# Sliding-window attention with an MLP-Mixer on one core: more dummy products at the start, evictions that lean to ScalarE only later, and new orders of PE's work and of the loads

## The chip, the cores and the metric

The kernel runs on one core of one Trainium2 chip. The metric is the device time of one execution in microseconds (us). Engines are named as in the profile: PE (TensorE, matrix products), PEld (its weight loads), DVE (VectorE), ACT (ScalarE), POOL (GpSimd) and SP (SyncE, which here only issues transfers).

## The reference

Attention over a sliding window with sink keys, then one MLP-Mixer layer on the merged heads:

```python
scores = scale * np.matmul(q, k.transpose(0, 1, 3, 2))       # q, k, v: [4, 8, 768, 64], scale = 1/8
keep = is_sink | in_window                                   # keys 0 to 3, or 0 <= row - key < 128
scores = np.where(keep, scores, -1000000000.0)
a = np.exp(scores - np.max(scores, axis=-1, keepdims=True))
x = (a / np.sum(a)) @ v, heads merged                        # [4, 768, 512]
h = np.maximum(xt @ w_tok1, 0.0) @ w_tok2                    # xt = x transposed; w_tok1 [768, 256], w_tok2 [256, 768]
u = x + h.transpose(0, 2, 1)
out = u + np.maximum(u @ w_ch1, 0.0) @ w_ch2                 # w_ch1 [512, 1536], w_ch2 [1536, 512]
```

Inputs and outputs are FP32; the kernel computes its products in BF16 and adds in FP32.

## The kernel before

**Tiles and stages.** The 32 heads are worked off as 16 pairs of two heads; pairs 0 to 3 make batch 0, and so on. For one pair, q and k (128 partitions by 768) are turned, so that the head's 64 channels lie on partitions; scores of keys against the queries of their window are formed in three groups (each a tile of two PSUM banks), ACT takes the exponential of each group (L692), and the values product with v and a column of ones (`pv`, two halves of three tiles of queries) gives sums and outputs, which DVE normalizes into x_sb (reciprocal L778, product L781). The four sink keys of a pair have a product of their own (`score_sinks`, L746). When the four pairs of a batch are there, its tokens are mixed (`mix_h`, `mix_u`, with w_tok1 and w_tok2) to u, u is turned, and the channels are mixed (`mix_channels`), by a scheme of seven products for eight, whose sums of weights (L1484) DVE forms from w_ch. DVE evicts the output tiles (L1276), and SP and ACT store them (L1286).

**How q and k come in.** Pairs 0 to 3: SP loads them in FP32 (`load_raw`, L136, tiles q_f and k_f), and ACT, DVE or POOL casts them into q_bf and k_bf (`copy`, L195 on ACT, L197 on DVE and POOL). From pair 4 on POOL's own transfers cast on the way (`load_cast`, L168 and L173). Pairs 0 to 7 are turned on PE (L159 for batch 0, L163 for batch 1) and copied out of PSUM into qT and kT, by ACT or DVE, in two halves each; pairs 8 to 15 are turned by DMA transpositions that SP issues (L555). v of every pair comes by `load_v` (POOL, L181, six buffers v_aug in turn) and the weights by `load_w` (POOL, L206).

**Masks.** In the first pairs PE adds the mask to the scores (a product of mask_add and the identity, before the scores of the group); later DVE (L711) or POOL (L703) masks what ACT has written.

**What sets the order.** PE's order is written out in the table `ORDERED`, in words such as `s5`: a letter for a stream and a unit's number in it. t: turning q (even) and k (odd) of pairs 0 to 3; m: the mask products; s: the score groups of pairs 0 to 3 with the sink scores among them; o: the sink rows and `pv` halves of batch 0 (o1 and o2 are pair 0, o3 and o4 pair 1, o5 and o6 pair 2, o7 and o8 pair 3); g and h: token mixing of batch 0's two halves; a: score groups from pair 4 on (a12 is the first of pair 8); v: the `pv` halves of those; w: turning by PE from pair 4 on; k: token mixing from batch 1 on; n: sink scores of later pairs; c, x and y: the channel products. The table `LOADS` sets the order of POOL's loads: q, k and v with the pair, t with w_tok1 or w_tok2, c and d with a quarter of w_ch1 or w_ch2. All these loads go through one queue.

What ACT, DVE, POOL and SP do, and when, is decided as the program is built by a planner, class `Plan`: it keeps a time for each engine (`plan.free`), and for each pending operation a list of the engines that can do it, with a cost for each. `other` takes the operation that could begin first and gives it to the engine where its end, by these costs, is earliest; 400 ns (`BIAS`) are added against DVE, so that ACT is favoured. The order in which the planner takes operations is the order in which each engine has them in its queue. `commit_pe` and `choose` give each PE unit its PSUM banks, four single ones ("mx") and two double ones ("sc"); a unit of turning holds a bank until the copies that read it are done.

**The start.** The first instructions of DVE are memsets: the tile of the sink values (L219), the tile `ones` (L220), mask_add (L241). `ones` is the first 512 columns of a kT buffer and feeds seven dummy products of 128 by 512 (`keep_warm`), which begin before any data has arrived, and whose result nobody reads. POOL builds the identity and the masks (L243 to L255) and then issues the load of pair 0's v.

## Time and profile before

| | us |
|---|---|
| median of three runs | 191.21 (191.1 to 191.54) |
| the profiled execution | 191.41 |
| its span (first to last instruction) | 189.7 |
| mean granted clock of TensorE | 0.998 |
| PE busy | 181.5 |
| DVE, ACT, POOL busy | 160.8, 112.1, 78.5 |
| first dummy product, first transposition | 2.07, 5.17 |
| first exponential (ACT L692) | 8.45 |
| first product with v (o1) | 14.50 |
| last wait of PE over 0.2 before the end (for x_sb) | ends 28.45 |
| first scores of pair 8 (a12) | 63.59 |
| last product ends, about | 186.4 |

Busy shares say which engine has most to do, the windows where it has gaps, the waits what it waits for there, and the chain of work that ended last which of these waits counted. In the rows of the timeline the number in brackets is the idle time just before, and behind the arrow stands what ended it; "ps" is a bank of PSUM.

### The profile page before, as it was taken

Reading aid. Unit: us, or ns where it says so; the run is one execution under the profiler, and the core shown is the slowest. Engines: PE = TensorE matmul, PEld = TensorE weight load, DVE = VectorE, ACT = ScalarE, POOL = GpSimd, SP = SyncE. Lnnn points to the kernel's source line nnn. Section 1 sums busy time; section 2 is a strip of 40 time slices with the busy share of each in tenths; the row PEclk is TensorE's granted clock in tenths of the full one; section 3 lists DMA queues with packets and bytes.
Section 4 is the critical chain, followed back from the end, with each engine's and each line's share of the span. In section 5 each row is a group of like instructions: output and inputs, shape, how many; then the busy total and the mean of one; then the engine's idle time right before and its main releaser. Section 6 shows DMA issues by size and latency. Waiting matters only on the chain.

```text
span 189.7 us, 5560 instructions
## 1 busy us (share of the span) xinstructions
PE 181.5 (96%) x2269; PEld 131.7 (69%) x2269; DVE 160.8 (85%) x343; ACT 112.1 (59%) x210; POOL 78.5 (41%) x122
## 2 busy tenths in 40 slices
PE   5889989999999999999999999999999999999992
PEld 1335758766777888766666788865578887668882
DVE  4766969997699999988999998879998968799882
ACT  4698978999974653858875711488842203773000
POOL 5938566374807989472804970150240000000000
PEclk9999999999999999999999999999999999999999
DMA  5999999999999999999999995431100145200035
GB/s 186 288 276 185 188 193 199 200 197 178 175 141 119 168 117 158 135 149 170 292 119 147 166 117 117 180 146 28 28 5 0 28 86 221 111 0 3 0 138 194
DMA packets 82600, 26.31 MB, mean 139 GB/s; under 512 B 70032, under 2 KB 80272, under 8 KB 82576
## 3 DMA queue, kind: packets, MB, share of 16 engines
q0 software_dynamic: 56864, 11.80, 82.8%
q1 hardware_dynamic: 25088, 13.64, 33.0%
q10 hardware_dynamic: 624, 0.53, 0.8%
q8 instruction: 17, 0.28, 0.6%
q14 instruction: 7, 0.06, 0.2%
HBM read 26.75 MB, written 6.29 MB: 174 GB/s over the span
## 4 chain that ended last, share of the span: by engine, by line
PE 87%; DMA 5%; ACT 2%; DVE 1%; issue 1%; POOL 1%; POOLq 0%
PE ps L188 85%; DMA v_aug<-in_v_dram 5%; ACT pT L692 2%; PE ps L191 1%; PE ps L163 1%; DVE x_sb L781 1%; PE ps L597 1%; ACT kT L195 0%; POOL mask_add L247 0%; POOL mask_add L251 0%; DVE pT L711 0%; DVE o_sb L1276 0%; ACT u_sb L195 0%; DVE recip L778 0%; POOL ident L244 0%
## 5 line engine op out<-in xcount | busy, mean ns | idle before, releaser
L692 ACT ACTIVATE pT<-ps 128x1024 bf16<-128x1024 f32 (+1 forms) x48 | 44.9, 963 | 20.1 <-PE ps L188 19.8
L195 ACT ACTIVATE parts<-ps 128x384 f32<-128x384 f32 x54 | 24.6, 490 | 18.0 <-PE ps L188 16.5
L188 PE MATMUL ps<-uT,w_ch 128*128 128x384 bf16 x168 | 33.7, 326 | 0.0
L1164 DVE CUSTOM_DVE_ANT_0 v1T<-ps,parts 128x384 bf16<-128x384 f32 x54 | 28.1, 552 | 6.4 <-PE ps L188 6.0
L188 PEld LDWEIGHTS <-v1T 128*128 128x128 bf16 x288 | 27.6, 98 | 4.4 <-issue 0.2
L188 PEld LDWEIGHTS <-w_ch 128*128 128x128 bf16 x204 | 19.1, 98 | 10.7
L201 ACT ACTIVATE v1T<-ps 128x384 bf16<-128x384 f32 x41 | 19.8, 497 | 9.4 <-PE ps L188 8.8
L188 PE MATMUL ps<-uT_sums,k_f 128*128 128x384 bf16 x108 | 23.5, 326 | 0.0
L188 PEld LDWEIGHTS <-v_sums 128*128 128x128 bf16 x216 | 20.8, 98 | 3.4 <-issue 0.2
L703 POOL TENSOR_SCALAR_AFFINE_SELECT pT<-pT 128x256 bf16<-128x256 bf16 (+1 forms) x20 | 11.6, 612 | 24.4 <-issue 14.6
L188 PEld LDWEIGHTS <-w_tok 128*128 128x128 bf16 x192 | 18.1, 98 | 4.3 <-issue 1.3
L1276 DVE TENSOR_TENSOR o_sb<-ps,u_sb 128x512 f32<-128x512 f32 (+1 forms) x32 | 17.3, 551 | 3.2 <-PE ps L188 3.2
L188 PEld LDWEIGHTS <-k_f 128*128 128x128 bf16 x144 | 13.6, 98 | 8.3 <-issue 0.6
L188 PE MATMUL ps<-q_f,v1T 128*128 128x256 bf16 x144 | 19.0, 273 | 0.0
L188 PE MATMUL ps<-w_ch,v1T 128*128 128x256 bf16 x144 | 18.8, 273 | 0.0
L188 PE MATMUL ps<-q_f,v_sums 128*128 128x256 bf16 x144 | 18.7, 273 | 0.0
L188 PE MATMUL ps<-v_aug,pT 128*128 128x65 bf16 x352 | 17.7, 194 | 1.0 <-DMA v_aug<-in_v_dram 1.0
L188 PEld LDWEIGHTS <-pT 128*128 128x128 bf16 x352 | 16.2, 98 | 3.0 <-DMA v_aug<-in_v_dram 1.5
L181 POOL DMA_DIRECT2D v_aug<-in_v_dram x16 | 16.5, 1037 | 3.2 <-PE ps L188 1.5
L781 DVE TENSOR_TENSOR x_sb<-ps,recip 128x384 bf16<-128x384 f32 x32 | 17.2, 550 | 0.4
L188 PEld LDWEIGHTS <-kT 64*64 64x64 bf16 (+2 forms) x343 | 7.9, 104 | 13.0 <-issue 9.0
L188 PE MATMUL ps<-qT,kT 64*64 64x192 bf16 (+2 forms) x336 | 15.5, 249 | 0.3 <-ACT pT L692 0.3
(91 smaller groups left out, 301.4 us busy)
## 6 DMA issues: line engine op xcount, KB each, us to landing
v_aug<-in_v_dram POOLq DMA_DIRECT2D x16, 192.0 KB, 10.3
w_ch<-in_moe_w_ch_dram POOLq DMA_DIRECT2D x8, 384.0 KB, 10.9
out_dram<-o_sb SPq DMA_DIRECT2D x6, 512.0 KB, 2.9
out_dram<-o_sb SPq DMA_DIRECT2D x10, 256.0 KB, 2.2
q_f<-in_q_dram SPq DMA_DIRECT2D x4, 384.0 KB, 5.1
k_f<-in_k_dram SPq DMA_DIRECT2D x4, 384.0 KB, 5.8
k_bf<-in_k_dram POOLq DMA_DIRECT2D x16, 96.0 KB, 7.6
q_bf<-in_q_dram POOLq DMA_DIRECT2D x16, 96.0 KB, 10.5
```

Of the source, the lines that this page charges most:

```text
L163: issue(nc.tensor.transpose(outs[x][ds(D * h, D), j], t[rows, h, j], ident[rows, rows]))
L181: in_order(nc.gpsimd.dma_start(out=v_aug.rearrange("p i t d -> p (i t) d")[:, :, 0:D], in_=v[b].rearrange("h s d -> (h s) d")[2 * hp * S:2 ...
L188: issue(nc.tensor.matmul(*args, skip_group_check=True, **kwargs))
L191: issue(nc.tensor.transpose(out, in_, ident))
L195: in_order(nc.scalar.activation(out, in_, AF.Copy))
L201: in_order(nc.scalar.activation(out, in_, AF.Relu))
L597: issue(nc.tensor.transpose(outs[x][columns], rows_by_columns[rows, columns], ident[rows, rows]))
L692: in_order(nc.scalar.activation(part(tiles["pT", p][:, :, ds(2 * g, 2)]), of_keys(tiles["ps_s", p, g])[:, :, 0:width(g)], AF.Exp, scale=scale,
L703: in_order(nc.gpsimd.affine_select(out=pt, in_=pt, compare_op=ALU.is_ge, fill=0.0, base=-n, pattern=[[0, nk], [1 - 2 * n, P]], channel_mul ...
L781: in_order(nc.vector.tensor_tensor(out=x_sb[b][:, ts(half, QH), ts(hp, 2 * D)].rearrange("p t (i d) -> p t i d", i=2), in0=tiles["ps_o", p ...
L1164: in_order(nc.vector._custom_dve(TENSOR_ADD_SAT, out=v1_of(i, half), in0=ps, in1=kept[:, n], s0=HUGE, s1=0.0,))
L1276: in_order(nc.vector.tensor_tensor(out=sb(*out), in0=tiles["ps_out", b, t0, key[0]], in1=in1(), op=ALU.add,))
```

## The change

It has five parts.

1. The tile `ones` is filled first of all, in two memsets (128 columns, then 384), ahead of the tile of the sink values. The dummy products are eight of 128 columns and then seven of 512, where there were seven of 512.
2. In `turn`, three more dummy products of 128 columns, in a bank of their own, follow the turning of pair 0's q, which is the first unit; its planned cost is 700 instead of 200.
3. The 400 ns against DVE count only from 25 us of planned time on (`LEAN_FROM`). Before that an operation goes to the engine where it ends first.
4. The planner's clock for PE begins at 4.9 us instead of 4.0.
5. `ORDERED` and `LOADS` are new throughout.

```diff
-        "t0-1 m0-1 s0-1 t2 m2 s2 t3 m3 s3 o0 m4 s4 t4 m5 t5 s5 o1-2 m6 s6 w0 m7 s7 t6 m8 t7 s8 o3-4 s9-10 w1 "
-        "s11-12 g0-1 o5-6 g2 a0 o7-8 a1 g3 w2 a2 h0-1 g4-5 h2-4 n0 a3-4 h5 g6 v0 h6 g7 h7 v1 w3 a5 c5 c3 c0 c8 "
...
-        "c21 c4 c9 v7 x0-1 c20 c18 y0 x2 k4 w5 a12 x6 k5 x3 x7 a13-14 x4 y3 x5 x10 n2 k6 y2 v8 x8 k7 a15 y4 x11 "
...
+        "t0 m0 t1 s0 m1 t2 s1 t3 m2 s2 m3 o0 s3 m4 s4 t4-5 m5 t6 s5 o1-2 m6 s6 w0 m7 t7 s7 m8 o3 s8 o4 s9-10 w1 "
+        "s11-12 g0 o5 g1 a0-1 o6-8 g2-4 w2 a2 h0-1 g5-6 n0 h2-5 a3-4 h6 g7 v0-1 h7 c1 c0 c11 c4 c8 w3 a5 w4 c7 "
...
+        "c23 x0 c22 v7 a12-13 x1 c18 w5 x2 x6 k4 x3 y0 k5 x4-5 k6 y3 a14 x7 n2 a15-16 y5 v8 x10 k7 y2 x8-9 x11 "
...
     LOADS = (
-        "q4 v1 k4 t1 v2 t2 v3 q5 k5 c2 q6 v4 k6 c3 c0 c1 k7 q7 v5 d3 d0 d2 k9 v6 k8 v7 d1 q8 v8 q9 k10 q12 v9 "
-        "q10 k12 k11 q11 v10 k13 v11 v13 q13 k14 q15 q14 v12 k15 v14 v15 "
+        "q4 v1 k4 t1 v2 v3 t2 q5 k5 q6 c2 v4 c0 v5 k6 q7 k7 c3 c1 d3 v6 q8 d2 k8 v7 d0 k9 d1 q9 v10 v8 k12 "
+        "q10 k10 v9 k11 q11 q12 q15 v11 k13 q13 k14 q14 v12 k15 v13 v14 v15 "
     )
...
+    in_order(nc.vector.memset(ones[:, 0:P], 1.0))
+    in_order(nc.vector.memset(ones[:, P:], 1.0))
     v_sink_f = t_pool.tile([P, 4, HS * 2], BF16, name="uT_sums").rearrange("p n x -> p (n x)").bitcast(FP32)
...
-    in_order(nc.vector.memset(ones, 1.0))
...
-    def keep_warm(n, slot):
-        ps = bank("mx", 4 * P, slot=slot)
+    def keep_warm(n, width, slot=None):
+        ps = bank("mx", width, slot=slot)
         for _ in range(n):
-            mm(ps, ones[:, 0:P], ones, start=True, stop=True)
-
-    keep_warm(7, 2 * NSC)
+            mm(ps, ones[:, 0:P], ones[:, 0:width], start=True, stop=True)
+
+    keep_warm(8, P, 2 * NSC)
+    keep_warm(7, 4 * P, 2 * NSC)
...
+    LEAN_FROM = 25000.0
...
-                e = min(op.cost, key=lambda e: at[e] + op.cost[e] + BIAS * (e == "DVE"))
+                e = min(op.cost, key=lambda e: at[e] + op.cost[e] + BIAS * (e == "DVE" and at[e] > LEAN_FROM))
...
             turn_rows(p, n, ps)
-
+            if first:
+                keep_warm(3, P)
+
+        first = p == n == 0
         readers = [[op] for op in done[name + "T", p]]
+        if first:
+            readers.append([])
...
-            270 if by_head(p) else 200, run, [done[name + "_bf", p]], {"mx": readers}, [op for r in readers for op in r],
+            270 if by_head(p) else 200 + 500 * first, run, [done[name + "_bf", p]], {"mx": readers},
+            [op for r in readers for op in r],
...
-    plan.free.update(PE=4000.0, ACT=3200.0, DVE=3900.0, POOL=5300.0)
+    plan.free.update(PE=4900.0, ACT=3200.0, DVE=3900.0, POOL=5300.0)
```

**DVE ahead of the first normalization.** Before: q_f_160 and k_f_160 are raw tiles of pair 2, qT2_317 is the turned q of pair 2, kTs the sink columns of k; the last two rows normalize pair 0's first half.

```order
L197 COPY kTs_147<-ps_94 64x4 x2
L197 CAST k_bf_286<-k_f_160 128x2x6x64
L197 COPY qT2_317<-ps_94 128x384 x2
L197 COPY kTs_147<-ps_94 64x4 x2
L778 RECIPROCAL recip_372<-ps_94 128x6
L781 TENSOR_TENSOR x_sb0_171<-ps_94,recip_372 128x3x128
```

After: q_f_171 and k_f_173 are q and k of pair 3, qT2_340 and kT2_111 belong to pair 2, qT2_378 to pair 3.

```order
L197 CAST k_bf_294<-k_f_169 128x2x6x64
L197 CAST q_bf_314<-q_f_171 128x2x6x64
L197 COPY qT2_340<-ps_94 128x384
L197 COPY kT2_111<-ps_94 128x384
L197 COPY kTs_156<-ps_94 64x4 x2
L197 COPY qT2_378<-ps_94 128x384
L197 CAST k_bf_396<-k_f_173 128x2x6x64
L787 RECIPROCAL recip_401<-ps_94 128x6
```

Both casts of pair 3 and half of pair 2's kT have come to DVE, and one half of pair 2's qT has left it for ACT.

**PE ahead of the first values product.** Before, the turning of pair 2's k is followed by s5 (pair 1's scores, from qT2_249) and o1 (v_aug0 is pair 0's v, pT its exponentials).

```order
L159 MATMUL ps_94<-ident_129,k_bf_286 128x64
L188 LDWEIGHTS kT1_110
L188 MATMUL ps_94<-qT2_249,kT1_110 128x256
...
L188 LDWEIGHTS pT_231
L188 MATMUL ps_94<-v_aug0_95,pT_231 128x65
```

After, the turning of pair 3's q (q_bf_314, t6) stands between the last mask product and s5 (here from qT2_261).

```order
L188 MATMUL ps_94<-mask_add_136,ident_138 128x384
L159 LDWEIGHTS q_bf_314
L159 MATMUL ps_94<-ident_138,q_bf_314 128x64
...
L188 LDWEIGHTS kT1_110
L188 MATMUL ps_94<-qT2_261,kT1_110 128x256
...
L188 LDWEIGHTS pT_240
L188 MATMUL ps_94<-v_aug0_95,pT_240 128x65
```

So t6 has moved ahead of s5, o1, o2 and two more score groups.

**POOL's loads and casts.** Before (v_aug_97 is pair 2's v and v_aug_98 pair 3's, w_tok_167 and w_tok_168 are w_tok1 and w_tok2, q_f and k_f pair 3's):

```order
L206 DMA w_tok_167<-in_moe_w_tok_dram 128x6x256
L181 DMA v_aug_97<-in_v_dram 128x12x64
L206 DMA w_tok_168<-in_moe_w_tok_dram 128x2x768
L197 CAST q_bf<-q_f 128x2x6x64
L181 DMA v_aug_98<-in_v_dram 128x12x64
L197 CAST k_bf<-k_f 128x2x6x64
```

After (w_tok_176 and w_tok_177 are w_tok1 and w_tok2):

```order
L206 DMA w_tok_176<-in_moe_w_tok_dram 128x6x256
L181 DMA v_aug_97<-in_v_dram 128x12x64
L181 DMA v_aug_98<-in_v_dram 128x12x64
L206 DMA w_tok_177<-in_moe_w_tok_dram 128x2x768
L168 DMA q_bf<-in_q_dram 128x2x384
```

Pair 3's v has moved ahead of w_tok2, and POOL has no casts left between its loads.

22 rows, old and new, of the table ORDERED are left out of this document.

## The prediction

> **What bounds the kernel now.** I read the page's busy shares first, then the windows, then the chain that ended last, and only then single rows.
>
> ```profile
> PE 181.5 (96%) x2269; PEld 131.7 (69%) x2269; DVE 160.8 (85%) x343; ACT 112.1 (59%) x210; POOL 78.5 (41%) x122
> ```
>
> ```profile
> core 0: us, PE busy (x) PEld busy (x) DVE busy (x) ACT busy (x) POOL busy (x), PEclk, DMA share, GB/s
> 0.00:10.00 10.00, 7.15 (x59) 2.88 (x61) 6.22 (x22) 5.72 (x12) 8.05 (x17) 1.00 0.91 239
> ...
> 20.00:25.00 5.00, 4.57 (x88) 3.31 (x84) 4.73 (x14) 4.29 (x8) 2.53 (x4) 1.00 1.59 191
> 25.00:30.00 5.00, 4.32 (x111) 3.62 (x112) 3.43 (x9) 4.27 (x10) 2.89 (x4) 1.00 1.58 192
> 30.00:40.00 10.00, 10.00 (x172) 7.46 (x170) 9.37 (x22) 9.19 (x20) 5.44 (x7) 1.00 1.45 197
> ```
>
> PE is busy for 96% of the span, and the windows show where the other 4% lies: before 30 us, and from 186 us on. The list of PE's waits from 28.4 to 186 us has one line:
>
> ```profile
> PE ps L188 <- DVE x_sb L781: 0.3, 1, 0.3
> ```
>
> ```profile
> 4.17 10.29 DMA v_aug<-in_v_dram
> ...
> 75.36 111.01 PE ps L188 x1090
> ```
>
> The chain (its first long step and its longest are shown) goes through the load of pair 0's v, issued by POOL at 4.17 and 10.29 under way, and from 75.36 on through PE alone, up to 186.4; the last eviction and the store follow. So the end is set by three things: how much PE work there is, how much of it is done by the time PE runs without a gap (28.45 us), and what new gaps come after that. The products that compute something are the same before and after; the tail (last unit y27) is the same too. **The sum is therefore a sum of PE gaps.**
>
> **Part 1: the dummy products (priced at 0).**
>
> ```profile
> 2.07 3.17 PE L188 MATMUL ps<-kT 128*128 128x512 bf16 x7 [2.07 <-DVE kT L220]
> 5.17 0.50 PE L159 MATMUL ps<-ident,q_bf 64*128 64x64 bf16 x12
> 5.72 0.50 PE L159 MATMUL ps<-ident,k_bf 64*128 64x64 bf16 x12
> 6.16 1.89 PE L188 MATMUL ps<-mask_add,ident 128*128 128x512 bf16 x4
> ...
> 8.46 0.34 PE L159 MATMUL ps<-ident,q_bf 64*128 64x64 bf16 x12
> ```
>
> The four mask products took 1.89 us here, about 0.43 from one to the next, and the twelve transpositions 0.50 at 5.72 but 0.34 at 8.46, so PE is slow until about 8 us; the granted clock of the first window, 1.00, does not show that. The dummies after: eight of a quarter of the width (0.11 each, an estimate from 0.43) and seven of 0.43 make 3.9 us. Their first operand is ready some 0.7 us sooner (the memset ahead of it is gone, and its own is a quarter as wide), so they run from about 1.4 to 5.3, where the first transposition started at 5.17. Three more (0.32) and pair 0's first mask (0.86) now stand ahead of pair 0's k transposition, which ends at about 7.4 at the slow pace, or 6.4 if PE speeds up before 5 us; its first exponential then starts between 7.3 and 8.5. In the profile it started at 8.45. That range, −1.1 to 0, is hidden: the first values product (o1, 14.50) waits 0.52 for v, which lands at 14.46 (4.17 + 10.29), and pair 3's q lands at 13.66, whatever PE did before. Were that cover gone, the part would be worth up to −1.1. The mask's memset on DVE ends about 0.07 later (one more instruction), and with it POOL's first load; I carry 0.07 as part of the range.
>
> **Part 2: pair 3's q moves to DVE and stands ahead of a copy (+0.46).**
>
> ```profile
> 13.14 1.02 DVE L197 COPY qT<-ps 128x384 bf16<-128x384 bf16 x2 [0.81 <-PE ps L159]
> 13.66 0.82 POOL L197 CAST q_bf<-q_f 128x768 bf16<-128x768 f32 x1 [3.19 <-DMA q_f<-in_q_dram]
> 14.50 0.36 PE L188 MATMUL ps<-v_aug,pT 128*128 128x65 bf16 x6 [0.52 <-DMA v_aug<-in_v_dram]
> 16.43 1.02 ACT L692 ACTIVATE pT<-ps 128x1024 bf16<-128x1024 f32 x1 [0.75 <-PE ps L188]
> 17.35 0.48 ACT L195 ACTIVATE qT<-ps 128x384 bf16<-128x384 bf16 x1
> 17.72 1.03 ACT L692 ACTIVATE pT<-ps 128x1024 bf16<-128x1024 f32 x1
> 18.63 0.89 ACT L195 ACTIVATE kT<-ps 128x384 bf16<-128x384 bf16 x2
> ...
> 21.19 0.34 PE L188 MATMUL ps<-qT,kT 64*128 64x256 bf16 x4 [0.33 <-ACT pT L692]
> ```
>
> The order of DVE shows the cast of pair 3's q ahead of the copy of pair 2's qT; PE's shows the transposition that reads this cast (t6) ahead of s5 and o1. q of pair 3 landed at 13.66: POOL's cast waited 3.19 us for exactly that. So DVE stands from there: cast 13.66 to 14.14 (DVE's back-to-back casts and copies lie about 0.5 apart: two copies in 1.02), copy to 14.7, t6 14.75 to 15.05 (the transpositions' 0.3), s5 to 15.33, and o1 at 15.33 instead of 14.50: **+0.83**. Queued behind that cast on DVE are the copies of pair 2's kT and of the sink columns; PE's later score groups wait for them, and so they shift with it.
>
> From o1 to the next exponential nothing is cut (14.50 to 16.43 before), so it starts at 17.26. From there ACT ends last: exponentials and three copies in a row up to the scores at 21.19, which waited 0.33 for ACT. One of the kT copies goes to DVE; one copy takes 0.37 from start to start (17.35 to 17.72). So s12 starts at 21.19 + 0.83 − 0.37 = 21.65: **+0.46**. Bounds: if the q lands up to 0.8 sooner or DVE's copy is no obstacle, 0.83 goes to 0 and the term is −0.37; if two copies stay on ACT, it is +0.83.
>
> **Part 3: two waits go (−0.86).**
>
> ```profile
> 24.52 0.38 PE L188 MATMUL ps<-qT,kT 64*64 64x256 bf16 x8
> 25.41 0.36 PE L188 MATMUL ps<-v_aug,pT 128*128 128x65 bf16 x6 [0.51 <-DMA v_aug<-in_v_dram]
> 28.45 0.38 PE L188 MATMUL ps<-x_sb,w_tok 128*128 128x256 bf16 x2 [0.27 <-DVE x_sb L781]
> ```
>
> The first of the two waits is for pair 3's v. Two answers on the tile v_aug give the landings: the load issued at 8.74 (pair 2's) took 13.5 us, so 22.2, and the one at 14.43 (pair 3's) 10.9, so 25.3. Between them landed the second token weight:
>
> ```profile
> DMA to landing us min/median/max: 13.5/13.5/13.5
> ```
>
> ```profile
> DMA to landing us min/median/max: 10.9/10.9/10.9
> ```
>
> ```profile
> L206 POOL DMA_DIRECT2D w_tok<-in_moe_w_tok_dram x2: 706/780/854, 7.9 to 9.8; - x2
> ...
> DMA to landing us min/median/max: 12.8/13.4/14.1
> ```
>
> 9.8 + 14.1 is 23.9. The queue hands over one load after the other, some 1.5 us each, and after the change pair 3's v stands ahead of that weight: v at about 23.9, the weight at about 25.4. PE's order fits it: o7–o8 now ask for v after g1 and a0–a1, at about 24.5, and g2–g4, the first to need the second weight, come behind o8, at about 25.8. Margins are 0.4 to 0.6, thin but positive. The second wait, for x_sb of pair 3, goes because g4 and the rest of batch 0 (0.66 more PE work than before) stand between o8 and h0. The price: eight score products took 0.89 to the next start here (24.52 to 25.41), and 0.30 where nothing was missing (63.59 to 63.89, in the rows of R3), so 0.59 goes; of the second the recorded 0.27. **−0.86** together; ends 0 (both waits come back elsewhere) and −0.86.
>
> **Part 4: the load list and the order from 30 to 186 us (taken as 0).** Nothing waits there before, so it can only lose. LEAN_FROM changes which engine evicts only before 25 us, whose effect is parts 2 and 3. I followed each first use of a late load: the w_ch quarters and k of pair 7 have margins of 0.5 to 1 us, by landings some 1.5 to 1.9 apart. The narrowest place is the rival below. Ends: 0 and +2.0.
>
> **Sum.** 0 + 0.46 − 0.86 + 0 = −0.4. The profiled execution took 191.41 (span 189.7 and 1.7 around it), so 191.0 beside it; the median of the runs shown is 191.21, 0.2 lower, so **190.8**.
>
> **The rivals.**
>
> *R1, DVE is not held up.* If o1 starts at 14.5 as before, part 2 is −0.37 instead of +0.46, and the time is about 190.1. Against it stands the row in which POOL waited 3.19 us for this very q.
>
> *R2, the change doesn't do what it says.* The dummies are hidden anyway, and the margins of part 3 are 0.4 to 0.6: if loads land half a microsecond later than reckoned, the waits come back at o7 or g2 and give −0.4 back: 191.2.
>
> *R3, the slower side: the scores of pair 8 catch up with their transposition.* Pairs from 8 on are transposed by DMA from SP.
>
> ```profile
> 59.18 1.46 PE L188 MATMUL ps<-uT,w_ch 128*128 128x384 bf16 x8
> 60.48 1.47 PE L188 MATMUL ps<-w_ch,v1T 128*128 128x256 bf16 x12
> 61.79 1.47 PE L188 MATMUL ps<-x_sb,w_tok 128*128 128x256 bf16 x12
> 63.19 0.58 PE L597 MATMUL ps<-ident,u_sb 64*64 64x64 bf16 x48
> 63.59 0.36 PE L188 MATMUL ps<-qT,kT 64*64 64x256 bf16 x8
> 63.89 0.28 PE L188 MATMUL ps<-q_f,v_sums 128*128 128x256 bf16 x1
> ```
>
> ```profile
> L555 SPq DMA_TRANSPOSE kT<-k_bf x8: 1210/1358/2983, 48.4 to 114.8; - x8
> ...
> DMA to landing us min/median/max: 7.0/7.9/8.8
> ```
>
> ```profile
> L173 POOL DMA_DIRECT2D k_bf<-in_k_dram x2: 821/824/828, 40.5 to 41.8; - x2
> ...
> DMA to landing us min/median/max: 9.1/9.3/9.6
> ```
>
> a12, pair 8's first scores, started at 63.59. In the new order x1 (six products, half of the 1.31 that twelve take), c18 (half of the 1.30 from 59.18 to 60.48), y0 and x2 (twelve products, 60.48 to 61.79, 1.31), k4 (1.40) and w5 (0.40) stand behind it: 4.4 us, so a12 is due at 63.6 − 4.4 − 0.4 = 58.8. Its k landed at 41.8 + 9.1 = 50.9; the new list has one w_ch quarter and k of pair 9 fewer ahead of it and q of pair 8 more, that is one quarter, about 1.9 us: 49.0. A stall begins where the transposition takes over 58.8 − 49.0 = 9.8 us. The rows give 7.0 to 8.8; with one slow issue ahead on SP (2.98) 10.9 for the median and 11.8 for the longest: a stall of 1.1 to 2.0, all of it lost, since PE has no gap to catch up in. About 192.3.
>
> *R4, DVE holds up POOL's loads.* More casts run on DVE while POOL issues loads.
>
> ```profile
> L181 POOL DMA_DIRECT2D v_aug<-in_v_dram x16: 1014/1033/1143, 4.2 to 105.5; - x16
> ```
>
> If each of the casts and copies that DVE takes over before 25 us (one cast, two or three copies) cost a load its 0.5 us, v of pair 3 would come up to 0.8 later than reckoned, the gain of part 3 would go: 191.6. Against it: of sixteen issues the shortest took 1014 ns and the longest 1143, the first ones with DVE busy for 6.22 of 10 us beside them, so a load lost 0.13 at most; and the loads land 10 us and more behind their issue, so the queue has work. The Trainium skill, page "SBUF — State Buffer", section "Who interferes with whom", says that a copy or cast on DVE in a two-port mode locks GpSimd out of the shared port for the whole instruction, and that loads issued by GpSimd then wait for their descriptors; by that rule the change would be slower, and the issue times quoted here speak against it.
>
> **How the numbers follow.** Forecast, 190.3 to 191.0: 0.45. R1: 0.10. R2: 0.15. R3: 0.25. R4: 0.05. A measurement of this kernel can tell about 0.2% (0.38 us) from no change, so faster means under 190.83: R1 and most of the forecast, 0.33 of its 0.45; within 0.2%: the rest of the forecast, 0.12, and R2; slower: R3 and R4. That makes 0.43, 0.27, 0.30. The range runs from R1 (190.1) to the middle of R3 (192.4) and leaves out about 2 in 10. The likeliest case's own range is 190.3 to 191.0.
>
> **What would show it.** Part 1: the first exponential between 7.3 and 8.5, dummies ending at about 5.3. Part 2: t6 at about 14.75 and o1 at about 15.3 with DVE as the releaser, the s12 scores at about 21.6. Part 3: no wait of PE for v_aug after 20 us and none for x_sb near 28. Part 4: PE's waits from 29 to 186 stay below 0.3 in sum; R3 shows as a wait of the scores for kT near 59. The prediction is wrong if the sum of PE's gaps behind 29 us passes 0.5, or if the early gaps don't shrink.

## The result, and the profile after

The changed kernel takes 193.56 us (median of four runs, 193.38 to 194.47), the kernel before beside it 191.38: a ratio of 1.0117, with a 95% interval of 1.0074 to 1.0161. Run twice more on other chips, twelve times each, it came out at 1.0053 (1.0030 to 1.0077) and 1.0063 (1.0034 to 1.0092). It is slower in all three; by how much differs, since single executions of either kernel spread over 2 to 3 us (the kernel before from 190.84 to 193.31 in one set). Executions more than 1.5% above the fastest one of the same kernel are left out of the ratios. The forecast was 190.8 and faster: wrong in sign.

The profiled execution of the changed kernel took 193.55, with a span of 191.6 (before: 191.41 and 189.7). Its busy times, windows and waits, in the views that the prediction showed of before:

```profile
PE 181.8 (95%) x2278; PEld 132.7 (69%) x2280; DVE 163.8 (85%) x351; ACT 112.7 (59%) x213; POOL 72.0 (38%) x112
```

```profile
core 0: us, PE busy (x) PEld busy (x) DVE busy (x) ACT busy (x) POOL busy (x), PEclk, DMA share, GB/s
0.00:10.00 10.00, 6.57 (x65) 3.00 (x66) 6.09 (x22) 6.28 (x11) 8.03 (x17) 1.00 0.88 230
...
20.00:25.00 5.00, 4.79 (x104) 3.41 (x101) 4.58 (x13) 4.86 (x8) 2.79 (x3) 1.00 1.55 195
25.00:30.00 5.00, 5.00 (x125) 4.40 (x122) 4.49 (x11) 4.41 (x9) 2.88 (x4) 1.00 1.59 191
30.00:40.00 10.00, 10.00 (x216) 7.51 (x215) 9.02 (x22) 9.32 (x21) 6.27 (x8) 1.00 1.46 197
60.00:80.00 20.00, 18.73 (x293) 15.35 (x293) 18.40 (x37) 10.41 (x17) 16.19 (x21) 1.00 2.41 146
```

```profile
PE ps L188 <- DVE o_sb L1285: 1.0, 1, 1.0
PE ps L188 <- DVE u_sb L940: 0.3, 1, 0.3
```

The gap between 25 and 30 us is gone (4.32 busy before, 5.00 now), as forecast. In its place stands one where there was none: 18.73 of 20 from 60 to 80 us, and the waits from 28.4 us on name it: 1.0 and 0.3 for evictions by DVE. The last eviction, in a row of each chain (before, then after), starts 1.23 later; the span is 1.9 longer, so another 0.67 lies behind it, in the stores:

```profile
186.39 0.42 DVE o_sb L1276
```

```profile
187.62 0.42 DVE o_sb L1285
```

**The sum of the difference.** From the 1400th to the 1200th product from the end (the same 200 products in every variant of the changed order) PE took 14.18 us, from 58.80 to 72.98; in two variants in which it waits for nothing there, it took 12.68 (e1 and f3, below). So the middle lost 1.50. The last eviction is 1.23 later; all the rest up to there gained 0.27. In us: −0.27 up to 60 and after 72, +1.50 between, +0.67 in the tail, +0.24 outside the span (193.55 − 191.6 against 191.41 − 189.7): +2.14, the whole difference of the two profiled executions. Of the −0.27, −0.16 is there by 35 us, where both kernels have done the same units of PE (35.02 against 35.18).

**The middle.** The chain that ended last, and DVE and PE in the timeline:

```profile
58.66 7.86 DMA kT<-k_bf
66.52 0.02 issue
66.55 0.16 DVE kTs L197
```

```profile
66.55 0.75 DVE L197 COPY kTs<-kT 64x4 bf16<-64x4 bf16 x2 [0.82 <-DMA kT<-k_bf]
67.33 0.76 DVE L1239 TENSOR_TENSOR v_sums<-v_sums,v1T 128x1152 bf16<-128x1152 bf16 x1
68.01 0.69 DVE L1285 TENSOR_TENSOR o_sb<-ps,o_sb 128x512 f32<-128x512 f32 x1
68.61 0.42 DVE L1285 TENSOR_TENSOR o_sb<-ps,u_sb 128x256 f32<-128x256 f32 x1
69.08 0.81 PE L188 MATMUL ps<-q_f,v_sums 128*128 128x256 bf16 x6 [0.97 <-DVE o_sb L1285]
71.54 0.55 PE L188 MATMUL ps<-qT,kT 64*64 64x256 bf16 x16 [0.30 <-DVE u_sb L940]
```

The sink columns of pair 9 are copied out of its k, which a DMA transposition turns. Its load (issued at 46.19) landed at 58.5, the transposition was issued at 58.66 and landed at 66.52. The planner gave the two small copies to DVE, and DVE stood idle 0.82 us ahead of them. Behind them in its queue are the evictions that free PE's banks, and PE waits for the second one.

**The tail.** Section 3 of the page has the fetches of instructions as a queue of their own; first before, then after:

```profile
q8 instruction: 17, 0.28, 0.6%
```

```profile
q8 instruction: 18, 0.29, 0.7%
```

That the fetches of this queue are PE's is inferred from the experiments below, where their place follows the number of PE's instructions. The eighteenth begins at 184.86 us in the trace: 16 KB, 1.45 us, just as the last seven stores are issued. The landing of the o_sb stores from 184.3 us on, before and after:

```profile
DMA to landing us min/median/max: 2.1/2.1/2.2
```

```profile
DMA to landing us min/median/max: 3.0/3.0/4.0
```

### The profile page after: what moved, and what is told of

The parts are those of the page before. It is cut to its first block, busy times and chain, and to the rows that moved or that the text cites. A ratio compares the mean times of both kernels' runs of the same rounds, so it can differ in the third digit from the quotient of the medians.

```text
span 191.6 us, 5597 instructions
## 1 busy us (share of the span) xinstructions
PE 181.8 (95%) x2278; PEld 132.7 (69%) x2280; DVE 163.8 (85%) x351; ACT 112.7 (59%) x213; POOL 72.0 (38%) x112
## 4 chain that ended last, share of the span: by engine, by line
PE 81%; DMA 10%; DVE 3%; ACT 2%; issue 1%; ACTq 0%
PE ps L188 79%; DMA kT<-k_bf 4%; DMA q_f<-in_q_dram 4%; DMA uT_sums<-in_v_dram 2%; ACT pT L701 2%; DVE o_sb L1285 1%; PE ps L163 1%; PE ps L191 1%; DVE v_sums L1239 1%; DVE u_sb L940 1%; DVE kTs L197 0%; DVE qT L197 0%; PE ps L600 0%; DVE uT_sums L221 0%; ACT qT L195 0%
## 5 line engine op out<-in xcount | busy, mean ns | idle before, releaser
L188 PE MATMUL ps<-uT,w_ch 128*128 128x384 bf16 x168 | 34.6, 326 | 0.0
L1173 DVE CUSTOM_DVE_ANT_0 v1T<-ps,parts 128x384 bf16<-128x384 f32 x54 | 28.7, 553 | 4.0 <-PE ps L188 3.3
L188 PE MATMUL ps<-w_ch,v1T 128*128 128x256 bf16 x144 | 18.2, 273 | 0.0
L712 POOL TENSOR_SCALAR_AFFINE_SELECT pT<-pT 128x256 bf16<-128x256 bf16 (+1 forms) x20 | 10.5, 559 | 18.1 <-issue 16.7
L188 PEld LDWEIGHTS <-kT 64*64 64x64 bf16 (+2 forms) x354 | 9.1, 105 | 11.0 <-issue 8.7
```

Source lines behind the costliest of these rows:

```text
L188: issue(nc.tensor.matmul(*args, skip_group_check=True, **kwargs))
L712: in_order(nc.gpsimd.affine_select(out=pt, in_=pt, compare_op=ALU.is_ge, fill=0.0, base=-n, pattern=[[0, nk], [1 - 2 * n, P]], channel_mul ...
L1173: in_order(nc.vector._custom_dve(TENSOR_ADD_SAT, out=v1_of(i, half), in0=ps, in1=kept[:, n], s0=HUGE, s1=0.0,))
```

## The experiments

Each is timed against the kernel before on the same chip; the number is the ratio with its 95% interval. "Tail" is the time from the start of the last eviction to the end of the span, "PE fetches" the fetches of queue q8 within the span, "middle" what PE lost against 12.68 us from the 1400th to the 1200th product from the end. Both are read from the one profiled execution, which need not be a typical one.

| kernel | ratio | last eviction | tail | PE fetches | middle |
|---|---|---|---|---|---|
| before | 1 | 186.39 | 3.31 | 17 | |
| g4, before again | 0.9985 (0.9959 to 1.0011) | 188.12 | 3.30 | 17 | |
| f2, before, 11 dummies more | 1.0020 (0.9995 to 1.0045) | 186.73 | 3.97 | 18 | |
| f4, before, dummies early | 1.0021 (0.9988 to 1.0054) | 186.15 | 3.84 | 18 | |
| h1, before, v3 first | 1.0013 (0.9980 to 1.0047) | 186.41 | 3.31 | 17 | |
| i2, h1 with q8 sooner | 0.9990 (0.9959 to 1.0022) | 186.46 | 3.30 | 17 | |
| after | 1.0117 (1.0074 to 1.0161) | 187.62 | 3.97 | 18 | 1.50 |
| a1, after again | 1.0053 (1.0030 to 1.0077) | 186.89 | 4.03 | 18 | 0.25 |
| h3, after again | 1.0063 (1.0034 to 1.0092) | 188.52 | 3.78 | 18 | 2.00 |
| e1, copies on POOL | 1.0071 (1.0046 to 1.0095) | 187.59 | 4.04 | 18 | 0.00, then 1.07 near 86 us |
| e2, sink memset sooner | 1.0065 (1.0041 to 1.0089) | 186.96 | 3.76 | 18 | 1.34 |
| e3, tail's order of before | 1.0073 (1.0050 to 1.0095) | 187.29 | 3.75 | 18 | 1.60 |
| f1, dummies joined | 1.0054 (1.0026 to 1.0081) | 187.23 | 4.01 | 18 | 1.56 |
| f3, copies behind evictions | 1.0036 (1.0010 to 1.0063) | 185.50 | 4.23 | 18 | 0.00 |
| g1, seven dummies | 1.0044 (1.0015 to 1.0074) | 187.07 | 3.28 | 17 | 0.04 |
| g2, g1 and f3 | 1.0059 (1.0029 to 1.0090) | 186.66 | 3.30 | 17 | 0.50 |
| g3, g2, sink memset first | 1.0011 (0.9986 to 1.0036) | 186.54 | 3.31 | 17 | 0.90 |
| h2, k9 ahead of d0 | 1.0185 (1.0117 to 1.0254) | 188.45 | 4.08 | 18 | 0.00, but 1.9 lost before it |

### The tail: stores that bunch, or one fetch more

The first theory of the tail was that the new order of the last output products issues the stores too close together. a1 and e3 were made for it, f1, f2 and g1 for the second theory.

a1 is the changed kernel, unaltered.

> The changed kernel once more, unaltered, for a second profile beside the variants. Theory 'stores bunch': the time from the end of the last eviction to the end of the span is again about 3.5 us, with the last stores taking about 3 us each, where the kernel before had 2.9 and 2.1. Rival 'chance of one execution': it falls back to the 2.9 of before, and the span to about 190.9. In both, PE's wait of 1.0 near 69 us (for an o_sb eviction) comes back; if that is gone too, the reading of the first profile is wrong.

The tail is 4.03 again, so it was no chance. The middle's wait is not there again, though: it lost 0.25 instead of 1.50, with PE 0.5 later at the 1400th product. That part of my first reading needed correcting.

e3 puts the end of PE's order back:

```diff
-        "c149 x44 x43 x46 y21 x45 x48 x47 x49 y23-24 x50 x52-53 x51 y26 x54-55 y25 y22 y27"
+        "c149 x43 x46 x44 x48 y21 x47 y23 x49 y24 x50 x52-53 y26 x45 x54 x51 x55 y25 y22 y27"
```

> The changed kernel, with the last thirty words of PE's order (the output products of the last batch) in the order that they have before. Theory 'stores bunch': the stores are issued spread again, the last ones land in about 2.1 us instead of 3.0, the time from the last eviction to the end of the span falls from 3.5 to 2.9, and the time by 0.5 to 0.8, to about 192.8. Rival: the longer tail has another cause (the state of the queues, chance): tail and time unchanged within 0.2.

The stores were spread as before, and the tail stayed at 3.75, with eighteen fetches. "Stores bunch" falls.

f1 joins the dummies (12 PE instructions fewer than in the changed kernel, 10 more than before):

```diff
-    keep_warm(8, P, 2 * NSC)
-    keep_warm(7, 4 * P, 2 * NSC)
+    keep_warm(3, P, 2 * NSC)
+    keep_warm(8, 4 * P, 2 * NSC)
...
-                keep_warm(3, P)
+                keep_warm(1, 3 * P)
```

> The changed kernel, with its dummy products joined: 3 of 128 columns, 8 of 512, and one of 384 after pair 0's q, instead of 8, 7 and 3 of 128, 512 and 128. The dummies take as long as in the changed kernel (4.0 and 0.3 us), but PE's program is 12 instructions shorter. Theory 'one fetch more': the changed kernel's 22 more PE instructions make PE fetch an eighteenth block of instructions at 184.9 us, 16 KB through one DMA engine for 1.4 us, just as the last stores run; all stores behind it land late, and the time from the last eviction to the end of the span is 4.0 instead of 3.3. If 12 instructions are enough to fall short of that block, the fetch is gone, the last stores land in about 2.1 us, and the tail is 3.3: 0.7 less. If they are not enough, fetch and long tail stay together. Rival 'stores bunch': the tail stays at 4.0 with no fetch in it. Up to 185 us nothing changes in either.

Twelve were not enough: fetch and long tail are both still there.

f2 goes the other way: the kernel before, whose seven dummies are cut into eighteen.

```diff
-    keep_warm(7, 2 * NSC)
+    keep_warm(14, P, 2 * NSC)
+    keep_warm(4, 4 * P, 2 * NSC)
```

> The kernel before, with its seven dummy products of 512 columns cut into 18 (14 of 128 and 4 of 512, 3.2 instead of 3.0 us long), so that PE's program has the 22 instructions more that the changed kernel has, and nothing else changes. Theory 'one fetch more': an eighteenth fetch of PE instructions near 184 us, the last stores land in about 3 instead of 2.1 us, the tail grows from 3.3 to 4.0, the time by 0.6 to 0.8. Rival 'stores bunch' (the order of the last output products): tail and time as before.

Nothing but 22 PE instructions at the start was added, and at the other end of the program the tail grew from 3.31 to 3.97, with this row on its page and these landings from 184.3 us on:

```profile
q8 instruction: 18, 0.29, 0.7%
```

```profile
DMA to landing us min/median/max: 2.8/3.0/3.1
```

g1 is the changed kernel with seven dummies of 512 columns, as many as before, and none after pair 0's q:

```diff
-    keep_warm(8, P, 2 * NSC)
     keep_warm(7, 4 * P, 2 * NSC)
...
-            if first:
-                keep_warm(3, P)
```

> The changed kernel with seven dummy products of 512 columns (as many as before, in one piece, from about 1.55 to 4.6 us) and none after pair 0's q, so that PE's program has exactly as many instructions as before; all orders are the changed kernel's. Theory 'one fetch more': no fetch of PE instructions behind 171 us, the last stores land in 2.1 to 2.3 us, and the time from the last product's start to the end of the span is 3.6 as before instead of 4.3: 0.7 less. Rival 'stores bunch, by the new order of the last products': still 4.2 or more. Early, PE may speed up later than in the changed kernel (8 instead of 5 us), which should cost at most 0.5 by the first product with v.

Seventeen fetches, and with the changed order of the last products the tail is 3.28:

```profile
q8 instruction: 17, 0.28, 0.6%
```

```profile
DMA to landing us min/median/max: 2.1/2.1/2.2
```

The table has eighteen profiles: with eighteen fetches the tail is 3.75 to 4.23 (eleven of them), with seventeen 3.28 to 3.31 (seven). In the profiles the cause is shown in both directions: PE instructions added at the start bring the longer tail, taken away they remove it, whatever the order of the last products. In four of the seven (g4, h1, g2 and i2) the trace has an eighteenth fetch too, but it begins 0.6 to 1.1 us behind the end of the span; so what the added instructions do may be to bring a fetch sooner, ahead of the last stores, and not one more. In the ratios the 0.67 us (0.35%) is not resolved: f2's interval holds it and holds no change as well, and g1's overlaps a1's. That the fetch delays the stores by holding one DMA engine for 1.45 us fits its row, but was not tried apart from the fetch itself.

g4 is the kernel before once more.

> The kernel before, unaltered, for a second profile. Theory 'one fetch more': again no fetch of PE instructions behind 171 us and 3.6 us from the last product's start to the end of the span. If the tail is 4.2 here too, the tail of the first profile was chance. Early waits and landings show how far one kernel's executions differ (a few tenths).

Its tail is 3.30. Its other rows say why executions spread: PE waited 1.9 us for pair 0's v here (o1 at 15.55), 0.5 in the first profile (o1 at 14.50), and for pair 3's v, which cost 0.5 there, it did not wait:

```profile
15.55 0.36 PE L188 MATMUL ps<-v_aug,pT 128*128 128x65 bf16 x6 [1.91 <-DMA v_aug<-in_v_dram]
```

That execution (193.41) was the slowest of its nine.

### The middle: the head of DVE's queue, or late loads

e1 and f3 take the two copies out of the evictions' way.

```diff
-                    copy(e, ks[ds(D * i, D), i, c:c + n_sink], kT[ds(D * i, D), 0:n_sink])
+                    copy("POOL" if p == 9 else e, ks[ds(D * i, D), i, c:c + n_sink], kT[ds(D * i, D), 0:n_sink])
```

> The changed kernel, with only the two copies of pair 9's sink columns (kTs from the DMA-turned kT) on POOL instead of DVE, at the same place in the program. Theory 'head of the queue': in the changed kernel these copies wait on DVE until 66.5 us for a DMA transposition, and the evictions queued behind them free PE's banks late; on POOL they hold up only loads, so PE's waits near 69 and 71 us (1.0 and 0.3) go and the time falls by 1.2 to 1.4, to about 192.2. Rival 'the late transposition itself': whoever reads pair 9's turned k waits for it wherever the copy runs, the wait moves to the sink scores near 70.8 us, and the time stays within 0.3 of 193.5. Second rival: POOL's masks or loads, now behind the copies, make PE wait later (193 and more).

In its profile there is no wait near 69 us, and the middle lost nothing. But POOL took 0.88 us for the copies, its loads behind them (k, q and v of later pairs, near 68 us) were issued 1.6 us later than in a1, 0.75 of which lay ahead of the copies already, and at 86.92 us PE waited for a transposition, for which this is the one line of its waits from 55 to 90 us:

```profile
PE ps L188 <- DMA qT<-q_bf: 0.7, 1, 0.7
```

It lost 1.07 there from start to start: the last product started at 187.28, as in the changed kernel. That is what the second rival said, though only a part of POOL's delay comes from the copies.

f3 leaves them on DVE, three instructions further back:

```diff
+                if p == 9:
+                    deferred.append(lambda: sinks_now(e))
+                else:
+                    sinks_now(e)
...
+                    if deferred:
+                        passed.append(key)
+                        if len(passed) == 2:
+                            deferred.pop()()
```

> The changed kernel, with pair 9's two sink-column copies still on DVE, but queued three instructions later, behind the two evictions that PE waits for near 69 us. POOL and all other orders are as in the changed kernel. Theory 'head of the queue': no wait of 1.0 near 69 us, and, since POOL's loads are not held up as they were with the copies on POOL, no new wait near 87 us: the time falls by 1.0 to 1.4 against the changed kernel. Rival: the transposed k lands late whatever stands in the queue, and the wait moves to the sink scores or to the evictions behind the copies: within 0.3 of the changed kernel.

In its profile the evictions come first and the copies find their data (no idle time ahead of them); PE waits for nothing from 55 to 90 us, and the last eviction starts at 185.50, 2.1 sooner than in the changed kernel and 0.9 sooner than before:

```profile
65.42 0.68 DVE L1292 TENSOR_TENSOR o_sb<-ps,o_sb 128x512 f32<-128x512 f32 x1
66.02 0.41 DVE L1292 TENSOR_TENSOR o_sb<-ps,u_sb 128x256 f32<-128x256 f32 x1
66.35 0.35 DVE L197 COPY kTs<-kT 64x4 bf16<-64x4 bf16 x2
```

That execution (191.68) was the fastest of its ten, whose median is 192.77, a ratio of 1.0036 where the unaltered kernel has 1.0053 and 1.0063. The intervals overlap.

Neither profile tests the copies, though. The transposition of pair 9's k had landed at 64.88 in e1 and at 64.64 in f3 (66.52 in the changed kernel), and DVE was done with what stands ahead of the copies' old place at 65.36 and 64.75. At that place, too, they would have found their data, as they do in a1, g1 and h2, where they were not moved and the middle lost 0.25, 0.04 and 0.00. What ties a loss to the copies are the profiles in which DVE stood idle ahead of them, 0.82 us after the change, 0.78 in e2 and 0.90 in e3: in each of these PE then waited for the eviction behind them, 0.97, 0.49 and 0.88. That they are a cause there is read from the chain, not shown by an experiment, and they are not the whole. f1 lost its 1.56 mainly elsewhere, with DVE at the head of its queue for another load, and only 0.17 idle at the copies:

```profile
60.30 1.03 DVE L1493 TENSOR_TENSOR q_f<-w_ch 128x768 bf16<-128x768 bf16 x2 [2.49 <-DMA w_ch<-in_moe_w_ch_dram]
60.32 0.81 PE L188 MATMUL ps<-w_ch,v1T 128*128 128x256 bf16 x6 [0.66 <-DMA w_ch<-in_moe_w_ch_dram]
```

h2 exchanges two loads of the changed kernel's list, pair 9's k and w_ch2's first quarter, and leaves every other order as it is:

```diff
+    a, b = done["ch2", 0], done["k_bf", 9]
+    a.fn, b.fn = b.fn, a.fn
```

> The changed kernel, with the loads of pair 9's k and of w_ch2's first quarter exchanged in POOL's queue; every other engine's order is untouched, the copies still on DVE at the same place. Theory 'load list': pair 9's k lands about 2 us sooner (56.5 instead of 58.5), its transposition by about 64.5, and the copies on DVE find it there: no wait of PE for o_sb near 69 us; w_ch2's first quarter lands 1.3 later (about 61), and DVE's sums of weights near 60 us wait for it longer, so PE waits there for products with them (0.5 to 1.2). Altogether within 0.5 of the changed kernel: the loss moves from 68 to 60 us. Theory 'head of the queue alone': the wait near 69 goes, nothing takes its place, 0.5 to 1.4 less than the changed kernel.

Pair 9's k landed at 53.1, and the wait near 69 is gone. But DVE now stood 2.84 us at the head of its queue for the quarter of w_ch2, and PE waited 1.75 for a u_sb queued behind it:

```profile
56.65 1.03 DVE L1493 TENSOR_TENSOR q_f<-w_ch 128x768 bf16<-128x768 bf16 x2 [2.84 <-DMA w_ch<-in_moe_w_ch_dram]
60.48 0.81 PE L188 MATMUL ps<-uT,w_ch 128*128 128x384 bf16 x4 [1.75 <-DVE u_sb L940]
```

So the loss moved, as the theory of the load list had it; the size did not fit. The three executions that enter the ratio took 194.4, 194.73 and 196.92; their median is 1.8 above that of h3 on the same chip, and the profiled one was the fastest. What the slowest of them lost besides is not in any profile, and stays open.

h3 is the changed kernel a third time.

> The changed kernel once more, on the chip of h1 and h2, for a third profile: an eighteenth fetch and a tail of about 4.3 from the last product's start, and between 60 and 72 us a loss between 0.2 and 1.5, the larger the earlier PE comes there (losses so far: 1.5 where the 1100th product from the end started at 58.8 less the waits, 0.3 where PE was 0.5 later).

It lost 2.0 in the middle, with these four waits (1.4 in sum), two of them for a load or a transposition itself and two for DVE, which had stood 2.68 us for w_ch near 61 us and 0.73 at the copies:

```profile
PE ps L188 <- DMA w_ch<-in_moe_w_ch_dram: 0.6, 1, 0.6
PE ps L188 <- DMA kT<-k_bf: 0.3, 1, 0.3
PE ps L188 <- DVE u_sb L940: 0.3, 1, 0.3
PE ps L188 <- DVE o_sb L1285: 0.2, 1, 0.2
```

Three profiles of one program: 1.50, 0.25 and 2.00. The rule I had put into the expectation, the earlier PE comes the more it loses, does not hold (h3 came there as a1 did, and lost eight times as much). What differs beside it is when the loads land: pair 9's k at 58.5, 58.2 and 59.9, with PE's 1400th product from the end at 58.80, 59.32 and 59.20.

### The start

e2 puts the sink values' memset between the two of the dummies' operand.

```diff
     in_order(nc.vector.memset(ones[:, 0:P], 1.0))
-    in_order(nc.vector.memset(ones[:, P:], 1.0))
...
     in_order(nc.vector.memset(v_sink_f, 0.0))
+    in_order(nc.vector.memset(ones[:, P:], 1.0))
```

> The changed kernel, with the memset of the sink values' tile put between the two memsets of the dummies' operand instead of behind both, so that the four small loads of sink values are issued at about 1.6 instead of 2.06 us. Theory 'shared slots': SP's loads of pair 3 waited for the slots of these small loads (issued at 6.65 instead of 5.46), so pair 3's q landed at 14.18 instead of 13.66; with them sooner, q lands at 13.7 to 13.9, the first product with v starts 0.3 to 0.5 sooner than 15.87, and the time falls by 0.2 to 0.5. Rival: pair 3's q is late because the DMA engines are busier, whoever issues; then it lands at 14.2 as before and the time stays within 0.15.

In the profile the theory held. In the changed kernel's chain SP's load of pair 3's q is issued at 6.65, as the sink values' load of 2.06 has landed; the two share a semaphore in the trace. In e2 it is issued at 5.55 and cast at 13.70 instead of 14.20:

```profile
2.06 4.57 DMA uT_sums<-in_v_dram
6.63 0.02 issue
6.65 7.53 DMA q_f<-in_q_dram
```

```profile
13.70 0.56 DVE L197 CAST q_bf<-q_f 128x768 bf16<-128x768 f32 x1 [1.03 <-DMA q_f<-in_q_dram]
```

Two more profiles go the same way: with the first sink values' load at 2.06 (f4) SP's load is issued at 6.33, with it at 1.51 (g3) at 5.40. PE was 0.5 ahead of the changed kernel from there to 59 us, 0.2 at 63 us, and 0.7 behind the wait near 69, which was 0.49 instead of 0.97. The time did not follow: 1.0065 against 1.0053 for a1 on the same chip.

f4 is the kernel before with the first part of the change alone (`ones` first, eight dummies of 128 and seven of 512).

> The kernel before with the first part of the change alone: dummies' operand first on DVE, eight products of 128 and seven of 512 columns; orders, lean and the rest as before (16 more PE instructions). Forecast of the prediction: hidden, within 0.2 of before up to 185 us. Theory 'shared slots': the sink values' loads are issued at 2.06 instead of 1.51, pair 3's loads get their slots later, pair 3's q and k land 0.5 or more later; since the old order asks for them later, PE after 30 us is at most 0.3 behind. PE speeds up about 3 us sooner (mask products 0.22 apart by 6 us), and the first exponential starts near 7.5. With an eighteenth fetch the tail is 4.0, without it 3.3.

The first exponential starts at 7.83, and the last product 0.24 sooner than in the first profile of before; the fetch takes 0.53 in the tail. Nothing is left that the interval can tell from before. So the dummies' own gain is hidden or small, as forecast, and in this profile their length in instructions costs more.

g2 and g3 put the mended parts together.

> As g1, and pair 9's sink-column copies stand behind two evictions on DVE. If both theories hold, tail and middle are both mended: no wait of PE over 0.5 from 60 to 80 us, tail 3.6, and against the changed kernel 1.5 to 2.0 us less: about 0.3 to 0.8 below the kernel before (ratio 0.996 to 0.999). If the middle is late transpositions rather than the queue's head, waits come back at other places and the ratio stays above 1.002.

> As g2, with the memset of the sink values' tile first on DVE again, as in the kernel before (dummies from 2.07 us). By the theory of shared slots pair 3's q lands 0.3 to 0.5 sooner than in g2 and the time is 0.2 to 0.5 below g2; PE speeds up near 8 us as in the kernel before, which, if the start of the products with v hangs on loads alone, costs nothing. If g3 is slower than g2, the early speed-up is worth more than the loads.

g2 has the short tail and lost 0.50 in the middle, and is still at 1.0059: a miss. g3, which differs in one memset, is at 1.0011, and cannot be told from before; it lost 0.90 in the middle, to w_ch. That the memset makes the step from g2 to g3 is not shown, since their intervals overlap. Taken together, mending the tail, the copies and the sink values brings the new orders back to the old time, and no further.

### Part 3 alone, and where its gain goes

h1 is the kernel before with pair 3's v loaded ahead of w_tok2, and g2, the unit that needs w_tok2 first, behind o8.

```diff
-        "... g0-1 o5-6 g2 a0 o7-8 a1 g3 w2 ..."
+        "... g0-1 o5-6 a0 o7-8 g2 a1 g3 w2 ..."
...
-        "q4 v1 k4 t1 v2 t2 v3 q5 ..."
+        "q4 v1 k4 t1 v2 v3 t2 q5 ..."
```

> The kernel before with part 3 of the change alone: pair 3's v is loaded ahead of w_tok2, and PE's unit g2, the first to need w_tok2, stands behind o7 and o8 instead of ahead of them; nothing else of the two tables changes, nor the dummies, nor the lean. Forecast of the prediction's part 3: pair 3's v lands at about 23.9 instead of 25.4, the wait of PE for it (0.5 in one profile, 1.9 in the other of the kernel before) goes, and 0.4 to 1.0 us with it: ratio 0.995 to 0.998. Rival: g2 now waits for w_tok2, which lands at about 25.4, for as long, and the time stays within 0.2 of before.

By the 1600th product from the end h1 was 0.81 ahead of before (41.00 against 41.81). Then, at the scores of pair 8:

```profile
63.68 0.38 PE L188 MATMUL ps<-qT,kT 64*64 64x256 bf16 x8 [0.73 <-DMA qT<-q_bf]
```

Before, the same scores started at 63.59, with no wait. The transposition of pair 8's q had landed there at 63.46, just in time. In h1 it was issued 0.84 sooner (58.25 against 59.09) and landed at 63.64, so the whole gain was given back in this execution. It need not be: in f4, with the order of before, the transposition landed at 62.24, and the 0.47 that PE was ahead of before by then was still there at the 1100th product from the end. Neither the forecast nor the rival (g2 waiting for w_tok2) named that place.

i2 loads pair 8's q sooner in h1 ("d2 k8 v6 q8 v7 d1 k9" for "d2 k9 v6 k8 v7 d1 q8").

> h1 (the kernel before with pair 3's v ahead of w_tok2), with pair 8's q loaded where pair 9's k stood, and pair 9's k behind w_ch2's second quarter: the list reads d2 k8 v6 q8 v7 d1 k9. Theory 'the load list paces PE': h1 gained 0.8 by 41 us and lost it at 63.7, waiting for the transposition of pair 8's q; with that q landed some 4 us sooner, the wait of 0.7 goes, and the last product starts 0.5 to 0.8 sooner than in h1 (185.3 to 185.6 in its profile, where h1 and before had 186.1), ratio 0.996 to 0.998. Rival: the next late load takes its place (w_ch2's second quarter, pair 7's v, or pair 9's transposed k near 70 us): the same total loss between 55 and 75 us, ratio 1.000 or above.

From 55 to 90 us PE waits for nothing. But pair 0's v came 0.7 later than in h1 (o1 at 15.05 instead of 14.37), so the last eviction starts at 186.46 all the same; the ratio, 0.9990 (0.9959 to 1.0022), allows the hoped gain as well as none. No version was shown to beat the kernel before.

## Why the prediction was wrong, step by step

**The bound.** "A sum of PE gaps" was the right frame: the gaps behind 29 us account for the loss up to the last eviction. Not seen was how little margin keeps the old kernel free of gaps there: the transposition for the scores at 63.59 landed at 63.46. A gap closed at 25 us can open again at the next late load (h1), and need not (f4).

**Part 1, the dummies, priced at 0.** The first exponential came at 7.43 (forecast 7.3 to 8.5) and was worth little (f4). In this profile PE's two mask products took 0.59 at 5.54, so it was fast by then; in the first profile of before, four took 1.89 at 6.16.

```profile
5.54 0.59 PE L188 MATMUL ps<-mask_add,ident 128*128 128x512 bf16 x2
7.43 1.02 ACT L701 ACTIVATE pT<-ps 128x1024 bf16<-128x1024 f32 x1 [0.26 <-PE ps L188]
9.01 1.07 DVE L197 CAST k_bf<-k_f 128x768 bf16<-128x768 f32 x1
```

That the dummies brought this is not shown: it is as much the luck of one execution. In the run g4 the unaltered kernel before was fast at 6.06, with its first exponential at 7.59, and in a1 the changed kernel was still slow at 5.81, with its own at 8.27 (g4, then a1):

```profile
6.06 1.04 PE L188 MATMUL ps<-mask_add,ident 128*128 128x512 bf16 x4
```

```profile
5.81 1.06 PE L188 MATMUL ps<-mask_add,ident 128*128 128x512 bf16 x2
```

The Trainium skill, page "TensorE: Matmul & The Clock Gate", section "What's actually happening", gives full speed once a free-running window of 3.4 us has been busy, so that the point varies from run to run; the traces agree, with PE busy from 1.13 and fast by 5.5 (after) or only behind 6.2 (a1), and busy from 2.07 and fast at 8 (before) or by 6.1 (g4). Two things were wrong. "Whatever PE did before", pair 3's q would land at 13.66: it landed at 14.18, since the memset that the dummies displaced holds up four small loads, which SP's loads wait for (one semaphore for both, e2). And the cost in length was not thought of: 22 instructions more, an eighteenth fetch ahead of the end, 0.67 in the tail.

**Part 2, +0.46.** The mechanism was there (o1 behind t6, t6 behind DVE's copy) and the size too small: o1 at 15.87 instead of 15.33, s12 at 22.24 instead of 21.65, so +1.05. Half a microsecond of it is the late q. Single executions differ as much: o1 started at 15.87, 16.39 and 16.27 in three of the changed kernel, at 14.50 and 15.55 in two of before. The first profile's rows for t6, o1 and s12:

```profile
15.40 0.33 PE L159 MATMUL ps<-ident,q_bf 64*128 64x64 bf16 x11 [0.39 <-DVE qT L197]
15.87 0.34 PE L188 MATMUL ps<-v_aug,pT 128*128 128x65 bf16 x6
22.24 0.34 PE L188 MATMUL ps<-qT,kT 64*128 64x256 bf16 x4 [0.21 <-ACT pT L701]
```

**Part 3, −0.86.** Right in kind, and too small: both waits are gone, and from s12 to h0 the changed kernel took 6.68 (22.24 to 28.92), where before took 7.26 (21.19 to 28.45) for 0.66 less of work (the unit g4 comes later there): −1.24 for the same work. h1, in which neither wait occurs, was 0.81 ahead of before, 0.13 of it by s12 already. The wait for pair 3's v is not in every execution of the kernel before: in the run g4, where PE came more than 1 us later, it is missing, and what h1's expectation counts as its 1.9 there is the wait for pair 0's v.

**Part 4, "taken as 0", and the tail, "the same".** These are the steps that failed. In the first profile the stretch from 60 to 72 us lost 1.50 and the tail 0.67, together the whole of the loss; the sign of being wrong that the prediction names, gaps over 0.5 in sum behind 29 us, came with 1.3. What stood in place of the 0 were evictions on DVE queued behind a copy that waits for a DMA transposition (read from the chain), and in place of "the same" an instruction fetch beside the last stores (f2, g1). The bound of +2.0 for part 4 held, the value chosen did not; "margins of 0.5 to 1 us" were reckoned from landings of one execution, while one program's middle lost 0.25, 1.50 and 2.00 in three.

**The rivals.** R3 had the sign and its kind, a DMA transposition that is waited for, and missed the place: pair 8's scores (a12) started at 59.43 without a wait; it was pair 9's sink columns, waited for on DVE. R1 went the other way (by its own terms its time would have been 190.0, not 190.1). R2 did not occur: the waits of part 3 stayed away. For R4, POOL's issues took no longer (1012 to 1142 ns); instead DVE's cast at 9.01 took 1.07, against 0.56 for the like one at 12.30, with POOL issuing two loads of v at 8.59 beside it (in the kernel before, the like cast at 8.20 took 0.94, so this is not new). That fits "Issue order, not op shape, decides who blocks" in the section of the Trainium skill cited with R4 (page "SBUF — State Buffer"), with DVE as the one blocked; no run here tried it.

**What stays open.** How much the tail, the copies, the late q and the load list each weigh in the median: each is seen in profiles, but the ratios of f3, g1 and g2 lie within each other's intervals. Whether moving the copies helps in an execution in which they would have waited: neither e1 nor f3 was one, and in g3 it would have been 0.3 us. What `LEAN_FROM` does by itself was not tried, since it changes the planner's whole order. And what h2's execution of 196.92 lost beside the profiled one.

## What to carry to other kernels

Before pricing an early gain, look for what PE next meets that is paced by something else, here the load queue: an engine without waits can be one whose loads land just in time, and then a gap closed early may only move. A small operation that waits for a transfer does not belong in front of evictions in an in-order queue. Count instructions as well as their time: dummies at the start brought a further instruction fetch ahead of the end, and that fetch fell on the last stores.

## What was not expected of the hardware

- An instruction fetch of PE (16 KB, 1.45 us) beside the last stores: they land in 2.8 to 4.0 us (after, f2) instead of 2.1 to 2.2 (before, g1), and the tail is 3.75 to 4.23 instead of 3.28 to 3.31, in eighteen profiles without an exception.
- Four loads of 2 KB each, issued by ACT 0.55 us later, held up a load on SP's queue by 1.2 (issued at 6.65 instead of 5.46), as the two use one semaphore.
- One program, three profiles: 1.50, 0.25 and 2.00 us lost in the same stretch, with landings of the same loads up to 1.7 us apart.
